# Head pair 0 of the first attention stage weighs its values in two halves of 128 tokens, and part of the early expert products is made from each half

## The chip, the cores and the metric

The kernel runs on one core of one Trainium2 chip. The metric is device microseconds (us) for one execution. Five engines work side by side, each through its own instructions in program order, and wait for each other through semaphores: PE (TensorE, matrix products), ACT (ScalarE), DVE (VectorE), POOL (GpSimd) and SP (SyncE, which here only issues DMAs). PE writes to PSUM; ACT and DVE read PSUM; the DMA queues move data between DRAM and SBUF.

## The reference, cut to what matters

Four batches of eight heads, 576 tokens, head width 64. Each query keeps its 32 best scores; the output feeds a mixture of eight experts whose gate is made doubly stochastic.

```
scores = q @ k.T / sqrt(64)                       # per batch and head, 576 x 576
keep the 32 largest per row, softmax over them    # attn
x = attn @ v                                      # 2304 x 512 after the heads are laid side by side
P = exp(x @ w_gate - max); 8 x: rows sum to 1, columns sum to 1, times N / E
out = sum over e:  P[:, e] * (relu(x @ w1[e]) @ w2[e])      # e = 0..7, 512 -> 1024 -> 512
```

Everything is float32. The row block of `x` that belongs to head pair `hp` (two heads, 128 columns) is `x[:, 128*hp : 128*hp + 128]`, so a product `x @ w1[e]` can be begun with the first head pair alone, as a sum over four such blocks.

## The kernel before, in words

Work is cut into blocks of 256 tokens. The attention of a block (a *stage*; the first is batch 0, tokens 0 to 255) goes head pair by head pair, `attend_heads`, L209, and inside a head pair by two *tiles* of 128 tokens, `weight_tiles`, L250: PE makes scores for each of the two heads (L122, L123, two matmuls for each half of the keys; the first tile of all in plain float32, L129), ACT copies them from PSUM (L134), DVE finds the 32nd largest by four MAX8 and three MATCH_REPLACE8 per head (L144, L147), ACT makes the exponentials (L150, L151), POOL and DVE normalise (L148, L199, L200, L203), PE transposes the weights in three groups of three blocks (L274) and ACT copies each group to the tile `at` (L291). When both tiles are in `at`, `weigh` (L301) multiplies by the values, 10 matmuls of 256 columns (L281), and ACT copies the result to `xt[:, hp, :]` (L304), from where it is split in a high and a low part (`xh` by ACT, L83; `xl` by DVE, L89).

Each expert product is made by three matmuls of such parts (L488 for the hidden layer, L601 for the outputs), and needs the block's four head pairs. To give PE something to do while the first stage is still under way, two functions make part of the hidden layer in plain float32 and store it in DRAM, where it is added later (`second_half`, L544):

- `first_quarter` (L516), called before head pair 1 is written out: for experts 4 to 7 the products with head pair 0 alone. For each expert four DMAs bring 128 rows of `w1` to a buffer `wr` (L520; three such buffers, `WR`, L48), and for each of four slices `s` two matmuls of 256 columns (L524) fill one bank of PSUM (`p1`, two buffers), ACT copies it to `y` (L512), SP stores `y` (L514).
- `first_half` (L528), called before head pair 2: for experts 0 to 3 the products with head pairs 0 and 1 (L537), four matmuls per slice.

Both are written at a low priority (`tc.high_priority(offset=-BIG)`, L367): a scheduler lays the instructions of each engine out in one fixed order before the run, by priorities and by a timeline of its own, and puts these matmuls where attention leaves PE free. Within an engine nothing overtakes at run time. After the first stage, `visit` (L567) takes one expert after the other over the blocks on board, and later attention stages are interleaved with it; `gate_logits` and `sinkhorn` make the gate; the last four blocks use a form with fewer products (L713, L775).

The names in the rows are tiles: `sp` scores in PSUM, `s` their copy, `m` the maxima, `Et` the weights, `pt` transposes or weighed values in PSUM, `p` a bank of expert products (`p_254` and the like in the lists of instructions: the stored part of one expert and slice), `raw`, `kh`, `kl`, `qs` the keys and queries, `wh`, `wl` weights in two parts.

Of the kernel before, what the change touches and what calls it, by code (L numbers as in the profile page):

```python
# [7 lines left out]
F32 = mybir.dt.float32  # L8
F32R = mybir.dt.float32r
U16 = mybir.dt.uint16  # L10
AF = mybir.ActivationFunctionType
# [4 lines left out]
DM, E, F = 512, 8, 1024  # L16
# [30 lines left out]
ALONE, LATER = range(0, 4), range(4, 8)  # L47
WR, WB, XR, NS, RAW, YB = 3, 6, 3, 3, 3, 4  # L48
# [3 lines left out]
def kernel(  # L52
# [11 lines left out]
    nc = tc.nc  # L64
    BIG = 1000000
# [3 lines left out]
    wp = ctx.enter_context(tc.tile_pool(name="wp", bufs=2))  # L69
    op_ = ctx.enter_context(tc.tile_pool(name="op", bufs=2))  # L70
# [3 lines left out]
    ps1 = ctx.enter_context(tc.tile_pool(name="ps1", bufs=2, space=PSUM))  # L74
# [3 lines left out]
    pst = actx.enter_context(tc.tile_pool(name="pst", bufs=2, space=PSUM))  # L78
    ap_ = actx.enter_context(tc.tile_pool(name="ap", bufs=2, side="right"))
    dram = ctx.enter_context(tc.tile_pool(name="dram", bufs=1, space=bass.MemoryType.DRAM))  # L80
# [35 lines left out]
    def scores(groups):  # L116
        sp = pss.tile([128, 2, 512], F32, name="sp")
        for dst, terms in groups:
            o = sp[:, dst[0], dst[1]:dst[2]]
            n = len(terms)  # L120
            for i, (qc, (kh, kl), cs) in enumerate(terms):
                nc.tensor.matmul(o, qc, kh[:, cs], start=(i == 0), stop=False)  # L122
                nc.tensor.matmul(o, qc, kl[:, cs], start=False, stop=(i == n - 1))  # L123
        return sp

    def plain_scores(qc, kr):
        sp = pss.tile([128, 2, 512], F32, name="sp")
        for a in range(2):
            nc.tensor.matmul(sp[:, a, 0:288], qc, kr[:, a * 288:a * 288 + 288], start=True, stop=True)  # L129
        return sp  # L130

    def copy_scores(sp):
        s = ap_.tile([128, S], F32, name="s", bufs=NS)
        nc.scalar.activation(s.rearrange("p (a b) -> p a b", a=2), sp, AF.Copy, scale=0.125)  # L134
        return s
# [111 lines left out]
        if not phases:  # L247
            attend_rest(hp, load_q("qm", 1024, 256, 1), ks, vr, xm)

    def weight_tiles(qs, ks, put, on_pool=False, crossed=None, plain=None):  # L250
        for t in range(2):
            Et = ap_.tile([128, 2, S], F32, name="Et", bufs=2)
            st = ap_.tile([128, 2, 2], F32, name="st", bufs=3)
            units = []
            for i in range(2):
                o = i * 256 + t * 128
                qc = qs[:, o:o + 128]
                if plain is not None and t == 0:
                    sp = plain_scores(plain[0][va if i == 0 else vb, o:o + 128], plain[1 + i][va if i == 0 else vb, :])
                else:  # L260
                    sp = scores([((a, 0, 288), [(qc, ks[i], slice(a * 288, a * 288 + 288))]) for a in range(2)])
                units.append((copy_scores(sp[:, :, 0:288]), Et[:, i, :], st[:, 0, i:i + 1]))
            topk(units, crossed is not None)
            normalise(Et, st, 2, on_pool)
            cs = slice(t * 128, (t + 1) * 128)
            if crossed is not None:
                cross(Et, crossed[:, :, cs])
                continue
            Ef = Et.rearrange("p a b -> p (a b)")
            for g in range(3):  # L270
                ps = pst.tile([128, 4, 128], F32, name="pt")
                for r in range(3):
                    j = g * 3 + r
                    nc.tensor.transpose(ps[:, r, :], Ef[:, j * 128:j * 128 + 128], idt)  # L274
                put(slice(g * 3, g * 3 + 3), cs, ps[:, 0:3, :])

    def weigh_values(av, vr, at, n, order):
        for j in order:
            for i, r in enumerate((va, vb)):
                o, block = (256 * i + 64 * j, 5 * i + j) if j < 4 else (512 + 64 * i, 4)  # L280
                weighed = nc.tensor.matmul(av[r, 0:n], vr[:, o:o + 64], at[:, block, 0:n], start=(j == order[0]), stop=(j == order[-1]))  # L281
        with tc.issue_after(weighed.ins):
            while ungated:
                gate_logits(*ungated.pop(0))

    def attend_phase(b, hp, qs, qm, ks, vr, xt, xm, plain=None):
        nq = 256 if xm is None else 320
        at = ap_.tile([128, 9, 320], F32, name="at", bufs=1)

        def put(blocks, cs, src):  # L290
            nc.scalar.activation(at[:, blocks, cs], src, AF.Copy)  # L291

        crossed = at if len(X) > 4 else None
        weight_tiles(qs, ks, put, b == 0 or crossed is not None, crossed, plain)
        if xm is not None:
            def put_rest(rows, blocks, src):
                nc.scalar.activation(at[rows, blocks, 256:320], src, AF.Copy)
            rest_weights(qm, ks, put_rest, None if crossed is None else at[:, :, 256:320])
        order = TAIL_FIRST if len(X) > 2 else range(5)

        def weigh():  # L301
            av = pst.tile([128, 512], F32, name="pt")
            weigh_values(av, vr, at, nq, order)
            nc.scalar.activation(xt[:, hp, :], av[:, 0:256], AF.Copy)  # L304
            if xm is not None:
                nc.scalar.activation(xm[:, hp, :], av[:, 256:320], AF.Copy)

        if turning:
            turning.append(weigh)
        else:  # L310
            weigh()
# [188 lines left out]


    PART = {}

    def half_weights(e, s2, half):
        wr = wp.tile([128, 2, 2, 256], F32, name="wr", bufs=WR)
        for r in range(2):
            nc.sync.dma_start(wr[:, r], w1[e, 2 * s2 + r, :, 2 * half:2 * half + 2, :])
        return wr

    def part(e, s, ps):  # L510
        y = op_.tile([128, 512], F32, name="y", bufs=YB)
        nc.scalar.activation(y, ps.rearrange("p a b -> p (a b)"), AF.Copy)  # L512
        PART[e, s] = dram.tile([128, 512], F32, name=f"p{e}_{s}")
        nc.sync.dma_start(PART[e, s], y)  # L514

    def first_quarter(x):  # L516
        for e in LATER:
            wr = wp.tile([128, 4, 256], F32, name="wr", bufs=WR)
            for s in range(4):
                nc.sync.dma_start(wr[:, s], w1[e, s, :, 0, :])  # L520
            for s in range(4):
                ps = ps1.tile([128, 2, 256], F32, name="p1")
                for fo in range(2):
                    nc.tensor.matmul(ps[:, fo, :], wr[:, s, fo * 128:(fo + 1) * 128], x[:, 0, :],  # L524
                                     start=True, stop=True)
                part(e, s, ps)
# [17 lines left out]
    def second_half(e, s, seat, wh, wl, k0):  # L544
        y = ap_.tile([128, 512], F32, name="yp", bufs=1)
        nc.sync.dma_start(y, PART[e, s])
        y = y.rearrange("p (a b) -> p a b", a=2)
# [333 lines left out]
```

## Time and profile before

| | us |
|---|---|
| median of 3 runs | 1831.21 (1831.04 to 1831.55) |
| profiled execution | 1833.39 |
| its span | 1831.6 |
| PE busy | 1785.6 (97%) |
| DVE, ACT, POOL busy | 1207.9, 1187.6, 1068.3 |
| DMA, mean rate | 148 GB/s |

The span runs from the first to the last instruction that the profiler recorded; 1.8 us of the profiled execution lie around it. A busy share is an average over stages. Two lines of the page cut the span in 40 slices of 45.8 us, each digit a tenth of busy time:

```
PE   4989999999999999999999999999999999999998
DVE  8999998988888878878787141255555555533333
```

Matmul durations overlap, since matmuls are pipelined; the pace of a run of equal matmuls is the distance of their starts. A row `x8` is eight matmul instructions; one float32 matmul of the code that has not been split in two parts is two instructions in the trace.

### The profile page before, as it was taken

How to read it: one execution, taken by the hardware profiler on the slowest of the kernel's cores; microseconds unless marked ns; L12 is line 12 of the kernel's file. 1: busy time of each engine (PE TensorE's matmuls, PEld its weight loads, DVE VectorE, ACT ScalarE, POOL GpSimd, SP SyncE). 2: the span in 40 equal slices, each digit the busy share in tenths (PEclk: the TensorE clock that was granted, in tenths of full speed). 3: DMA queues.
4: the chain of work that ended last, by engine and by line, in shares of the span. 5: the costliest groups of instructions: out<-in, count | busy, mean ns of one | idle time of the engine just before them, and what ended most of it. 6: DMA issues, size and time to landing. Idle time of an engine off the chain costs nothing.

```text
span 1831.6 us, 26304 instructions
## 1 busy us (share of the span) xinstructions
PE 1785.6 (97%) x9385; PEld 1480.7 (81%) x9385; DVE 1207.9 (66%) x2232; ACT 1187.6 (65%) x1785; POOL 1068.3 (58%) x842
## 2 busy tenths in 40 slices
PE   4989999999999999999999999999999999999998
PEld 3777888888888878777787889888888888888887
DVE  8999998988888878878787141255555555533333
ACT  5888899999999888988897645533333333333331
POOL 4367856656766585556564688955544554554441
PEclk9999999999999999999999999999999999999999
DMA  4885877765767575656655356423333333211111
GB/s 136 264 260 174 255 198 178 207 191 160 199 174 179 143 223 170 168 152 164 172 152 142 90 174 217 161 98 109 114 117 104 104 107 114 90 58 63 53 35 46
DMA packets 227203, 270.77 MB, mean 148 GB/s; under 512 B 142464, under 2 KB 146688, under 8 KB 227072
## 3 DMA queue, kind: packets, MB, share of 16 engines
q1 hardware_dynamic: 226928, 268.83, 49.8%
q8 instruction: 73, 1.20, 0.3%
q14 instruction: 58, 0.48, 0.1%
q10 hardware_dynamic: 144, 0.26, 0.0%
HBM read 202.19 MB, written 34.60 MB: 129 GB/s over the span
## 4 chain that ended last, share of the span: by engine, by line
PE 83%; ACT 4%; POOL 4%; DVE 3%; DMA 3%; issue 3%; SPq 0%; ACTq 0%; POOLq 0%
PE p L601 20%; PE p L775 19%; PE p L488 18%; PE p L713 10%; PE pc L713 5%; PE pt L281 4%; DMA wr<-in_w_dram 2%; PE pb L713 2%; POOL wl L86 2%; PE sp L122 2%; PE sp L123 2%; DVE m L144 1%; DVE w L147 1%; PE p L524 1%; ACT wh L83 1%
## 5 line engine op out<-in xcount | busy, mean ns | idle before, releaser
L86 POOL TENSOR_TENSOR wl<-wr,wh 128x1024 fp32r<-128x1024 f32 x288 | 694.0, 2422 | 456.2 <-ACT wh L83 445.7
L83 ACT ACTIVATE wh<-wr 128x1024 fp32r<-128x1024 f32 x288 | 304.1, 1061 | 284.4 <-PE p L713 191.2
L144 DVE MAX8 m<-w 128x8 f32<-128x576 f32 x432 | 320.6, 753 | 5.8
L488 PE MATMUL p<-xh,wh 128*128 128x256 f32 (+1 forms) x832 | 274.7, 330 | 2.8 <-DVE hl L557 1.9
L488 PE MATMUL p<-xl,wh 128*128 128x256 f32 (+1 forms) x832 | 273.7, 329 | 0.1
L488 PE MATMUL p<-xh,wl 128*128 128x256 f32 (+1 forms) x832 | 273.0, 328 | 0.0
L601 PE MATMUL p<-wh,hh 128*128 128x512 f32 x640 | 250.2, 396 | 4.3 <-ACT hh L556 2.8
L601 PE MATMUL p<-wl,hh 128*128 128x512 f32 x640 | 249.6, 392 | 0.0
L601 PE MATMUL p<-wh,hl 128*128 128x512 f32 x640 | 241.3, 392 | 0.0
L147 DVE MATCH_REPLACE8 w<-m,w 128x576 f32<-128x576 f32 x288 | 213.7, 743 | 0.0
L775 PE MATMUL p<-wh,h2h 128*128 128x512 f32 x512 | 199.1, 389 | 0.6 <-DVE acc L618 0.6
L775 PE MATMUL p<-wl,h2h 128*128 128x512 f32 x512 | 199.2, 389 | 0.0
L775 PE MATMUL p<-wh,h2l 128*128 128x512 f32 x512 | 196.3, 389 | 0.0
L618 DVE SCALAR_TENSOR_TENSOR acc<-p,P,acc 128x512 f32<-128x512 f32 x120 | 89.5, 750 | 160.4 <-PE p L775 160.4
L557 DVE SCALAR_TENSOR_TENSOR hl<-p,hh 128x512 fp32r<-128x512 f32 x160 | 109.0, 682 | 106.5 <-ACT hh L556 105.5
L488 PEld LDWEIGHTS p<-xh,wh 128*128 128x128 f32 x832 | 157.6, 189 | 20.8 <-issue 2.1
L488 PEld LDWEIGHTS p<-xl,wh 128*128 128x128 f32 x832 | 157.7, 189 | 15.7 <-issue 0.9
L488 PEld LDWEIGHTS p<-xh,wl 128*128 128x128 f32 x832 | 157.6, 189 | 14.2 <-issue 0.5
L144 DVE MAX8 m<-s 128x8 f32<-128x576 f32 x144 | 108.4, 753 | 85.3 <-ACT s L134 84.8
L601 PEld LDWEIGHTS p<-wh,hh 128*128 128x128 f32 x640 | 120.1, 188 | 31.7 <-ACT hh L556 5.3
L601 PEld LDWEIGHTS p<-wl,hh 128*128 128x128 f32 x640 | 120.6, 188 | 23.4 <-issue 0.4
L601 PEld LDWEIGHTS p<-wh,hl 128*128 128x128 f32 x640 | 119.9, 188 | 23.6 <-DVE hl L557 0.2
(171 smaller groups left out, 3550.4 us busy)
## 6 DMA issues: line engine op xcount, KB each, us to landing
wr<-in_w_dram SPq DMA_DIRECT2D x248, 512.0 KB, 3.5
y<-y SPq DMA_DIRECT2D x160, 256.0 KB, 2.8
raw<-in_k_dram SPq DMA_DIRECT2D x48, 288.0 KB, 3.7
p<-y SPq DMA_DIRECT2D x32, 256.0 KB, 4.0
wr<-in_w_dram SPq DMA_DIRECT2D x32, 256.0 KB, 4.3
yp<-p SPq DMA_DIRECT2D x32, 256.0 KB, 3.3
raw<-in_q_dram SPq DMA_DIRECT2D x31, 256.0 KB, 3.5
values<-in_v_dram SPq DMA_DIRECT2D x24, 256.0 KB, 3.6
```

The lines of the kernel that those rows point to most:

```text
L83: nc.scalar.activation(dst, src, AF.Copy)
L86: nc.gpsimd.tensor_tensor(dst, src, hi.bitcast(F32), op=OP.subtract)
L122: nc.tensor.matmul(o, qc, kh[:, cs], start=(i == 0), stop=False)
L144: nc.vector.max(m8[:, u, r, :], ws[u] if r else units[u][0])
L147: nc.vector.match_replace(ws[u], m8[:, u, r, :], ws[u] if r else units[u][0], LOWEST)
L281: weighed = nc.tensor.matmul(av[r, 0:n], vr[:, o:o + 64], at[:, block, 0:n], start=(j == order[0]), stop=(j == order[-1]))
L488: nc.tensor.matmul(ps[:, fo, :], a[:, kk, fs], x[:, k0 + kk, cs], start=(i == 0), stop=(i == 3 * nk - 1))
L557: nc.vector.scalar_tensor_tensor(seat.hl[:, ft, cs], src, 0.0, seat.hh[:, ft, cs].bitcast(F32), op0=OP.max, op1=OP.subtract)
L601: nc.tensor.matmul(ps, a[:, ft, ts], m[:, ft % 2, :], start=(i == 0), stop=(i == 3 * NFT - 1))
L618: return nc.vector.scalar_tensor_tensor(ACC[t], y, g, ACC[t], op0=OP.mult, op1=OP.add)
L713: nc.tensor.matmul(ps, w[:, kk, :], x[:, kk, :], start=(fresh and i == 0), stop=(i == 5), skip_group_check=True)
L775: nc.tensor.matmul(ps, a[:, ft, ts], m[:, ft, :], start=(i == 0), stop=(i == 11))
```

## The change

Only the call for the very first head pair changes (`plain is not None`), and the experts 5 to 7 of `first_quarter`.

- `weight_tiles` calls `then(t)` after each tile. In it, the values are weighed for that tile's 128 tokens alone (10 matmuls of 128 columns into a PSUM buffer of their own, in the order 0 to 4), and ACT copies 128 columns to `xt`. `weigh` is not called for this head pair.
- After tile 0, `first_eighths` loads the weights of experts 5, 6, 7 (the three `wr` buffers) and makes their products with the first 128 tokens: per expert two banks of PSUM with 8 matmuls of 128 columns, two copies by ACT, and four stores of 128 x 2 x 128 numbers, rows of 512 bytes.
- `first_quarter`, still called before head pair 1, makes the second 128 tokens of these three experts from the weights that are still in `wr`, then expert 4 as before.

```
+        if plain is not None:
+            def then(t):
+                av = pst.tile([128, 512], F32, name="pt")
+                weigh_values(av, vr, at, 128, range(5), t * 128)
+                nc.scalar.activation(xt[:, hp, t * 128:t * 128 + 128], av[:, 0:128], AF.Copy)
+                if t == 0:
+                    with tc.high_priority(offset=-BIG):
+                        first_eighths(xt)
+
+            weight_tiles(qs, ks, put, True, None, plain, then)
+            return
+        weight_tiles(qs, ks, put, b == 0 or crossed is not None, crossed)
...
+    QT = 3
...
+    SPLIT = []
+
+    def first_eighths(x):
+        for e in range(E - QT, E):
+            wr = wp.tile([128, 4, 256], F32, name="wr", bufs=WR)
+            for s in range(4):
+                nc.sync.dma_start(wr[:, s], w1[e, s, :, 0, :])
+            SPLIT.append((e, wr))
+            eighths(e, wr, x, 0)
+
+    def eighths(e, wr, x, t):
+        for s2 in range(2):
+            ps = ps1.tile([128, 2, 2, 128], F32, name="p1")
+            for r in range(2):
+                for fo in range(2):
+                    nc.tensor.matmul(ps[:, r, fo, :], wr[:, 2 * s2 + r, fo * 128:(fo + 1) * 128], x[:, 0, t * 128:t * 128 + 128],
+                                     start=True, stop=True)
+            y = op_.tile([128, 512], F32, name="y", bufs=YB)
+            nc.scalar.activation(y, ps.rearrange("p r a b -> p (r a b)"), AF.Copy)
+            for r in range(2):
...
+                nc.sync.dma_start(PART[e, 2 * s2 + r].rearrange("p (a b) -> p a b", a=2)[:, :, t * 128:t * 128 + 128],
+                                  y[:, r * 256:r * 256 + 256].rearrange("p (a b) -> p a b", a=2))
...
     def first_quarter(x):
-        for e in LATER:
+        for e, wr in SPLIT:
+            eighths(e, wr, x, 1)
+        for e in list(LATER)[:len(LATER) - QT]:
```

The scheduler lays all engines out anew. Three places show it; in these lists the number of matmuls is that of the code, and the lines of the changed kernel are 2 higher in `weight_tiles` and about 13 to 41 higher further down (L545 is the matmul in `eighths`, L283 the values, L548 the copy in `eighths`, L300 the copy to `xt` in `then`, L501 and L578 the matmuls that were L488 and L537).

PE before, from the last transposes of tile 0 of head pair 0 to the first values:

```order
L274 MATMUL pt<-idt,Et 128x128 x5
L122 MATMUL sp<-kh,qs 128x288
L123 MATMUL sp<-kl,qs 128x288
L122 MATMUL sp<-kh,qs 128x288
L123 MATMUL sp<-kl,qs 128x288
L274 MATMUL pt<-idt,Et 128x128 x9
L281 MATMUL pt<-at,values 64x256 x3
```

PE after, from the same transposes:

```order
L274 MATMUL pt<-idt,Et 128x128 x5
L283 MATMUL pt<-at,values 64x128 x10
L545 MATMUL p_196<-xt,wr 128x128 x4
L545 MATMUL p_207<-xt,wr 128x128 x4
L122 MATMUL sp<-kh,qs 128x288
L123 MATMUL sp<-kl,qs 128x288
L122 MATMUL sp<-kh,qs 128x288
L123 MATMUL sp<-kl,qs 128x288
L545 MATMUL p_223<-xt,wr 128x128 x4
L545 MATMUL p_234<-xt,wr 128x128 x4
L274 MATMUL pt<-idt,Et 128x128 x6
L545 MATMUL p_250<-xt,wr 128x128 x4
```

The values of tile 0 and 16 matmuls of the experts now stand between the transposes of tile 0 and those of tile 1, 8 of them ahead of the next scores.

ACT before, from the second weights of tile 1 of head pair 0 (`m_197`) to the scores of tile 1 of head pair 1:

```order
L150 ACTIVATE Et<-s,m_197 128x576
L151 ACTIVATE Et,st<-Et,eb 128x576 x2
L134 ACTIVATE s<-sp 128x576
L83 ACTIVATE kh<-raw 128x576
L83 ACTIVATE qs<-raw 128x512
L291 ACTIVATE at<-pt 128x3x128
L150 ACTIVATE Et<-s,m_420 128x576
L291 ACTIVATE at<-pt 128x3x128
L134 ACTIVATE s<-sp 128x576
```

ACT after, the same stretch (`m_290` and `m_468` are the same maxima):

```order
L150 ACTIVATE Et<-s,m_290 128x576
L300 ACTIVATE xt<-pt 128x128
L151 ACTIVATE Et,st<-Et,eb 128x576 x2
L134 ACTIVATE s<-sp 128x576
L548 ACTIVATE y<-p_196 128x512
L548 ACTIVATE y<-p_207 128x512
L83 ACTIVATE kh<-raw 128x576
L83 ACTIVATE qs<-raw 128x512
L548 ACTIVATE y<-p_223 128x512
L150 ACTIVATE Et<-s,m_468 128x576
L548 ACTIVATE y<-p_234 128x512
L293 ACTIVATE at<-pt 128x3x128 x2
```

One copy to `xt` stands ahead of the two L151, and four copies of expert products stand ahead of the next L134, which follows the last row shown.

PE before, where `first_half` ends and the first visit begins (head pair 3's values are the L281):

```order
L281 MATMUL pt<-at,values 64x256 x10
L537 MATMUL p_706<-xt,wr 128x256 x4
L122 MATMUL sp<-kh,qs 128x288
L123 MATMUL sp<-kl,qs 128x288
L122 MATMUL sp<-kh,qs 128x288
L123 MATMUL sp<-kl,qs 128x288
L274 MATMUL pt<-idt,Et 128x128 x3
L537 MATMUL p_715<-xt,wr 128x256 x4
L274 MATMUL pt<-idt,Et 128x128 x3
L488 MATMUL p_2844<-xh,wh 128x256
```

PE after, from the end of `first_half` on:

```order
L578 MATMUL p_763<-xt,wr 128x256 x4
L122 MATMUL sp<-kh,qs 128x288
L123 MATMUL sp<-kl,qs 128x288
L122 MATMUL sp<-kh,qs 128x288
L123 MATMUL sp<-kl,qs 128x288
L501 MATMUL p_2892<-xh,wh 128x256
L501 MATMUL p_2892<-xl,wh 128x256
L501 MATMUL p_2892<-xh,wl 128x256
L274 MATMUL pt<-idt,Et 128x128 x3
L283 MATMUL pt<-at,values 64x256 x3
```

The last of the early products now stands ahead of head pair 3's values, where before two groups of them stood behind.

## Rows read from the trace of the kernel before

**Rows 1.** The page, busy us of each engine, share of the span, instructions.
```profile
PE 1785.6 (97%) x9385; PEld 1480.7 (81%) x9385; DVE 1207.9 (66%) x2232; ACT 1187.6 (65%) x1785; POOL 1068.3 (58%) x842
```

**Rows 2.** Busy time by stretch: start:end, length, engines, granted clock, DMA share, GB/s.
```profile
30.40:44.40 14.00, 7.35 (x37) 4.70 (x37) 14.00 (x32) 9.84 (x21) 5.74 (x9) 1.00 0.29 81
44.40:70.50 26.10, 24.74 (x128) 19.86 (x129) 25.35 (x56) 22.23 (x47) 9.23 (x13) 0.93 0.74 244
70.50:118.40 47.90, 43.94 (x238) 35.99 (x236) 42.23 (x88) 38.21 (x76) 26.73 (x27) 0.96 0.85 275
118.40:160.00 41.60, 36.23 (x239) 29.73 (x239) 41.48 (x83) 34.32 (x64) 31.33 (x27) 0.93 0.65 213
160.00:800.00 640.00, 637.02 (x3811) 533.59 (x3808) 550.19 (x1087) 583.03 (x872) 417.54 (x361) 1.00 0.68 187
800.00:1600.00 800.00, 796.70 (x3909) 660.73 (x3910) 426.43 (x723) 417.00 (x586) 470.31 (x328) 1.00 0.43 130
```

**Rows 3.** PE in order of time: start, length, line, operation, count, idle before it.
```profile
29.09 1.27 PE L274 MATMUL pt<-idt,Et 128*128 128x128 f32 x5
...
34.70 0.61 PE L122 MATMUL sp<-kh,qs 128*128 128x288 f32 x1 [4.35 <-ACT s L134]
...
36.25 2.36 PE L274 MATMUL pt<-idt,Et 128*128 128x128 f32 x9 [0.22 <-POOL Et L203]
38.78 1.08 PE L281 MATMUL pt<-at,values 128*64 128x256 f32 x6 [0.16 <-ACT at L291]
...
44.41 0.40 PE L122 MATMUL sp<-kh,qs 128*128 128x288 f32 x1 [1.97 <-ACT s L134]
...
45.05 3.37 PE L524 MATMUL p<-xt,wr 128*128 128x256 f32 x8
...
57.31 1.89 PE L524 MATMUL p<-xt,wr 128*128 128x256 f32 x8
59.04 0.82 PE L274 MATMUL pt<-idt,Et 128*128 128x128 f32 x6
...
111.43 2.38 PE L281 MATMUL pt<-at,values 128*64 128x256 f32 x20
...
118.41 0.38 PE L488 MATMUL p<-xh,wh 128*128 128x256 f32 x1
```

**Rows 4.** ACT in order of time, same columns, around the first values.
```profile
31.83 0.77 ACT L150 ACTIVATE Et<-s,m 128x576 f32<-128x576 f32 x1 [0.94 <-DVE m L144]
32.51 0.76 ACT L151 ACTIVATE Et<-Et,eb 128x576 f32<-128x576 f32 x1
...
35.83 0.68 ACT L83 ACTIVATE kh<-raw 128x576 fp32r<-128x576 f32 x1 [1.18 <-PE sp L122]
...
38.62 0.65 ACT L134 ACTIVATE s<-sp 128x576 f32<-128x576 f32 x1
...
50.89 1.10 ACT L512 ACTIVATE y<-p 128x512 f32<-128x512 f32 x2
```

**Rows 5.** DVE in order of time, same columns.
```profile
40.09 0.74 DVE L144 MAX8 m<-s 128x8 f32<-128x576 f32 x1
...
89.26 0.76 DVE L144 MAX8 m<-s 128x8 f32<-128x576 f32 x1 [3.01 <-ACT s L134]
```

**Rows 6.** ACT in order of time, conversions of weights and head pair 3's values.
```profile
85.73 1.06 ACT L83 ACTIVATE wh<-wr 128x1024 fp32r<-128x1024 f32 x1 [3.65 <-DMA wr<-in_w_dram]
...
115.43 1.06 ACT L83 ACTIVATE wh<-wr 128x1024 fp32r<-128x1024 f32 x1 [2.91 <-DMA wr<-in_w_dram]
116.39 0.37 ACT L304 ACTIVATE xt<-pt 128x256 f32<-128x256 f32 x1
```

**Rows 7.** DMA issues: what, queue, count, KB each, median us to landing.
```profile
wr<-in_w_dram SPq DMA_DIRECT2D x16, 128.0 KB, 3.2
```

**Rows 8.** SP's queue in order of time: start, length with its waits, line, count.
```profile
31.28 7.36 SPq L230 DMA_DIRECT2D raw<-in_k_dram  x2
...
54.88 0.85 SPq L514 DMA_DIRECT2D p<-y  x2
```

More of the change, by code (lines that the diff above doesn't have):

```diff
@@ L248, in attend_heads, with weight_tiles @@
             attend_rest(hp, load_q("qm", 1024, 256, 1), ks, vr, xm)
-    def weight_tiles(qs, ks, put, on_pool=False, crossed=None, plain=None):
+    def weight_tiles(qs, ks, put, on_pool=False, crossed=None, plain=None, then=None):
         for t in range(2):
@@ L275, in weight_tiles, with weigh_values @@
                 put(slice(g * 3, g * 3 + 3), cs, ps[:, 0:3, :])
-    def weigh_values(av, vr, at, n, order):
+            if then is not None:
+                then(t)
+    def weigh_values(av, vr, at, n, order, c0=0):
         for j in order:
@@ L280, in weigh_values @@
                 o, block = (256 * i + 64 * j, 5 * i + j) if j < 4 else (512 + 64 * i, 4)
-                weighed = nc.tensor.matmul(av[r, 0:n], vr[:, o:o + 64], at[:, block, 0:n], start=(j == order[0]), stop=(j == order[-1]))
+                weighed = nc.tensor.matmul(av[r, 0:n], vr[:, o:o + 64], at[:, block, c0:c0 + n], start=(j == order[0]), stop=(j == order[-1]))
         with tc.issue_after(weighed.ins):
@@ L293, in attend_phase @@
         crossed = at if len(X) > 4 else None
-        weight_tiles(qs, ks, put, b == 0 or crossed is not None, crossed, plain)
+        if plain is not None:
[9 more added lines that the diff above has]
+        weight_tiles(qs, ks, put, b == 0 or crossed is not None, crossed)
         if xm is not None:
@@ L514, in part @@
         nc.sync.dma_start(PART[e, s], y)
+    SPLIT = []
[16 more added lines that the diff above has]
+            for r in range(2):
+                if (e, 2 * s2 + r) not in PART:
+                    PART[e, 2 * s2 + r] = dram.tile([128, 512], F32, name=f"p{e}_{2 * s2 + r}")
+                nc.sync.dma_start(PART[e, 2 * s2 + r].rearrange("p (a b) -> p a b", a=2)[:, :, t * 128:t * 128 + 128],
+                                  y[:, r * 256:r * 256 + 256].rearrange("p (a b) -> p a b", a=2))
     def first_quarter(x):
-        for e in LATER:
+        for e, wr in SPLIT:
+            eighths(e, wr, x, 1)
+        for e in list(LATER)[:len(LATER) - QT]:
             wr = wp.tile([128, 4, 256], F32, name="wr", bufs=WR)
```

## The prediction

> **What bounds the kernel now.** I read the page's busy shares first: PE 97% [rows 1], so the sum of what PE does and waits is the time. Then the busy time by stretch, to see where the 46 us that PE is not busy (1831.6 less 1785.6) lie [rows 2]. From 160 us to 1600 us PE is busy 1433.7 of 1440 us: there nothing but PE's own work counts, and all that a PE that arrives earlier needs is that the others keep up; DVE is busy 550 of 640 us in 160 to 800 and 426 of 800 after it, ACT 583 and 417. Between 30.4 and 44.4 us PE is busy 7.35 of 14.0, from 44.4 to 160 us 104.9 of 115.6; the last stretch, with the end of the run, is not touched. In these first 160 us DVE is the busy one (14.0 of 14.0, then 25.35 of 26.1, 42.23 of 47.9, 41.48 of 41.6): attention goes at DVE's pace, and PE fills up with early expert products. So the third view is PE in order of time [rows 3]: it stands idle for 4.35 us up to 34.70 and 1.97 us up to 44.41, both times for a copy of scores by ACT (L134), and the expert products begin only at 45.05, because they wait for head pair 0's two tiles. The change attacks these two gaps.
>
> One run stands for all numbers: the profiled execution took 1833.39 us, of which 1831.6 are the span; the median of the runs is 1831.21, 2.2 us less. I work out a difference on the trace and take it from the median.
>
> **Moved work: the gain.** Per 128 tokens an expert's quarter is 8 matmuls of the code, 16 instructions in the trace; three experts make 48 instructions that can run ahead of 44.41 instead of behind it. In full flow eight instructions of 256 columns take 59.04 - 57.31 = 1.73 us [rows 3], 0.216 each, so 0.108 for half the columns: 48 x 0.108 = 5.2 us. Before 44.41 there is room: 4.35 + 1.97 us idle, and half of head pair 0's value matmuls (about 1.2 of 2.4 us, rows of 20 in 2.38) moves from behind 38.78 to about 31 as well. So PE comes out of the early products 5.2 us sooner: **-5.2 us**.
>
> **Split matmuls: PE's extra.** The same columns are made by twice as many instructions: 96 of 128 columns for 48 of 256, and the weights are loaded twice. Streams alone say no extra (0.108 is half of 0.216). The nearest row with 128 columns and new 128 x 128 weights for each is the transposes, six in 0.82 us, 0.137 each, with the last one's full length in it [rows 3]: 96 x (0.137 - 0.108) = 2.8 us. I take 0, since the 0.82 holds a tail that a flow has once; ends 0 and +2.8. Less than nothing is excluded, as no column goes away. The values are 40 instructions of 128 columns for 20 of 256; they need the same columns: 0, with the same reason.
>
> The Trainium skill, page "TensorE: Matmul & The Clock Gate", section "Back-to-back issue gap", speaks against the change: it gives a sustained 81 ns per matmul at 128 columns and 131 at 512, so that narrow ones cost well over their share. An estimate from it: 98 at 256, two narrow for one wide 162, which makes 1.66 times of the 10.4 us that the three experts' 48 instructions take, +6.9 us. The trace's wide instruction (216 ns) and its transposes (at most 137) are far from such a ratio; that result is a rival below.
>
> **Moved on ACT: what hides it, and what not.** Six copies L548 come forward, 0.48 us each by the pair of L512 [rows 4], and the copy to `xt` is made in two pieces (one extra, 0.3 to 0.4). ACT is busy 9.84 of 14.0 us there [rows 2], so 3.2 us fit, but they stand in its order ahead of things that attention wants. The copy L300 stands ahead of the two L151. At PE's full pace the values of tile 0 (20 x 0.06 = 1.2 us) run 30.9 to 32.1, L150 ends at 32.5, L300 ends at 32.9: L151 comes 0.4 later than 32.51. Then two L548, keys, queries, L548, L150, L548 and two `at` copies follow before the L134 that stands at 38.62. Walked through with the rows' lengths (keys and queries 0.55 each, L150 0.68, `at` 0.4): scores end at 35.6, the keys' copy, at 35.83 before, starts at 36.0, L134 at 39.6, 1.0 later. Its copy ended at 39.27 and DVE took it up at 40.09 [rows 4, 5], a slack of 0.82. DVE is 0.2 late. At PE's slower pace (five transposes in 1.27 us at 29.09, nine in 2.36 at 36.25, about 0.25 each [rows 3]) the values take 2.4 us and the first 16 expert instructions 3.5, L151 slips by 1.2, and the same walk ends with L134 at 43.7, 5.1 us late, DVE 4.3 late. PE was quick at 38.78 after working since 34.70 with gaps of 0.2; in the new order it works from before 29.1 with only half a microsecond without work at 30.4, so it should be quick soon after 31. (The granted clock reads 1.00 over all of 30.4 to 44.4 [rows 2], though the pace is half in its first part; I go by the pace.) I take **+0.5**; ends 0 and 4.3. Behind 44.41 ACT has six such copies less, 2.9 us, in a stretch in which it is busy 22.23 of 26.1; I count no extra for it.
>
> **Stores, loads, SP.** 24 stores of 128 KB with rows of 512 bytes replace 12 of 256 KB with rows of 2 KB. Two issues take 0.85 us [rows 8], so SP spends about 12 x 0.43 = 5 us more, half of it before 44 us, where it mostly waits (7.36 us for two key loads, on POOL). The key and query loads of head pair 2 are now queued behind stores that wait for ACT's copies; by the walk above the second key load goes out at about 39, before at 38.6, and its converted keys are wanted after 50. The DMA engines are 0.29 busy in 30 to 44 [rows 2]. Nothing waits for the stores before the first visit. Expert 4's weights come when expert 5's buffer is free, about 47 to 48, landing 3.2 later [rows 7], at 51; PE gets there after six banks, 44.4 + 5.2 + some slow pace = 51. Cost 0; ends 0 and +1.
>
> **What is late next: head pair 3.** With early products used up 4.7 us sooner, PE comes to the first visit sooner, which needs head pair 3. Before, its values stood ahead of the last two groups of early products (111.43, L488 at 118.41); now they stand behind the last one (third pair of lists), so this cover is gone. In front of `xt` ACT stood 2.91 us for a weight's DMA at 115.43, as at 85.73 for 3.65 us, which cost DVE 3.01 us [rows 5, 6]. Those weights wait for `wr` buffers that early products free; if these end sooner, the loads start sooner, and `xt` of head pair 3 can be had 3 to 5 us sooner. At later equal points of attention (scores of the next stage's head pair 1 onward) the new order on PE has 4 to 6 us more work behind it than the old one. So I let the gain pass: 0; ends +4.7 (all lost) and -3 (DVE's stall of 3.01 goes too). Any change of the order past 200 us is worth nothing I can name.
>
> Sum: -5.2 + 0 + 0.5 + 0 + 0 = **-4.7 us**; the span would be 1826.9, the median **1826.5**. With the -3 for DVE and ACT's slip at 0.2: 1823.2.
>
> **The rivals.**
>
> 1. *The gain is lost at head pair 3* (1831.2). PE runs out of early products at about 113.7 and stands until `xh` and `xl` come at 118.4 as before. For it: the new order, in which scores, transposes and values lie between the last early product and the first visit's bulk. Against it: ACT's 2.91 us at 115.43 is a wait on a transfer, and DVE has 5.7 us without work in 70.5 to 118.4 [rows 2] that can shrink.
> 2. *ACT holds up DVE* (1835.5, slower). One mechanism: at PE's slow pace the copies of the first four banks, which stand ahead of L134, let DVE's next scores come 5.1 us late, beyond the slack of 0.82; DVE has no pause until 84 to win it back, each head pair is 4.3 later, and the first visit, for which PE has no cover left, begins 4.3 later: 1831.2 + 4.3. It decides from a slip of L134 above 0.82 us, and it is past 0.2% from a slip of 4.5. For it: PE is at the slow pace at 36.25, and again in 45.05 to 48.4 (eight instructions in 3.37 us) after an idle time of 1.97. Against it: the new order keeps PE at work from before 29.1.
> 3. *Narrow matmuls cost more than their columns* (1829.3 by the transposes' 0.137). The mechanism is the weight load of each instruction, which then sets the pace; only the nearest row's tail speaks for it. By the page above it would be 1833.4.
> 4. *More than the moved work is gained* (1823.2), as DVE's stall at 86 to 89 goes.
>
> That the change does not do what it says, I exclude: the list shows L545 ahead of tile 1's transposes.
>
> **How the numbers follow.** Forecast 0.50, rival 1 0.18, rival 2 0.13, rival 3 0.07, rival 4 0.12. About 0.2% (3.7 us) is what a measurement can tell from no change here. Within the forecast's own spread (1824 to 1829) 0.43 is beyond 3.7 us, 0.07 not; rival 4 adds 0.12 and rivals 1 and 3 together 0.04 to faster: 0.59. Same: 0.07, 0.15 of rival 1, 0.05 of rival 3, 0.02 of rival 2: 0.29. Slower: 0.11 of rival 2 and 0.01 of rival 3: 0.12. The range reaches from 1822.0 (rival 4 with one more microsecond) to 1833.0 (rival 1 with some of rival 2's slip); outside it lie most of rival 2 and a little of rival 4.
>
> **What would show it.** L545 starts at about 33 and its 48 instructions for tile 0 are done before 44; their starts are 0.11 apart in full flow (0.137 or more: rival 3). L134 for tile 1 of head pair 1 starts at 39 to 40 (43 or later: rival 2), and DVE has no gap over 0.5 us there. The first L578 comes 4 to 5 us ahead of where the first L537 was. The first visit's matmuls in flow come near 114 (118 or later with PE idle ahead of them: rival 1). In 160 to 1600 us PE's busy share stays as it is, with the whole shifted. It is wrong if the gaps of 4.35 and 1.97 us are filled, and the same time is idle between 100 and 160.

## The result: 0.7% slower, and the profile after

The changed kernel takes 1844.35 us (median of four runs, 1840.16 to 1848.88) against 1831.17 for the kernel before, run beside it: the ratio is 1.0073, 95% interval 1.0054 to 1.0092. (Ratios here are worked out over all runs of both kernels, so they can differ by up to 0.1% from those of the medians.) The forecast of 1826.5 with a range to 1833.0 does not hold it, and none of the four rivals does. The profiled execution is the one of 1848.88 us.

The page of the changed kernel, its span and the busy us of each engine:

```profile
span 1847.1 us, 26472 instructions
PE 1792.8 (97%) x9453; PEld 1486.7 (80%) x9453; DVE 1210.1 (66%) x2232; ACT 1189.1 (64%) x1786; POOL 1068.9 (58%) x842
```

PE is busy 7.2 us more than in [rows 1] and not busy 54.3 us, where it was 46. So of the 15.5 us by which the span is longer, 8.3 are idle time of PE and 7.2 are busy time: 68 more matmul instructions, and matmuls that take longer. Kernel e1 below, with the same 9453 matmul instructions in another order, is busy 1788.7 us, so about 4 of the 7.2 come with the order. The busy time by stretch, in the columns of [rows 2], says where:

```profile
30.40:44.40 14.00, 12.13 (x109) 10.41 (x107) 14.00 (x32) 12.83 (x29) 6.14 (x9) 1.00 0.43 118
44.40:70.50 26.10, 20.90 (x132) 16.32 (x133) 23.94 (x53) 20.08 (x42) 9.36 (x14) 1.00 0.81 241
70.50:118.40 47.90, 43.28 (x229) 34.88 (x229) 44.22 (x92) 38.95 (x75) 28.90 (x28) 0.96 0.87 285
118.40:160.00 41.60, 39.85 (x278) 33.40 (x275) 40.87 (x85) 35.48 (x67) 30.45 (x26) 1.00 0.62 193
160.00:800.00 640.00, 622.38 (x3639) 518.53 (x3638) 532.84 (x1047) 562.56 (x842) 403.44 (x348) 0.99 0.66 182
800.00:1600.00 800.00, 799.21 (x3974) 664.11 (x3973) 437.90 (x752) 430.70 (x608) 473.07 (x333) 1.00 0.45 134
```

The gap of 30 to 44 us is filled (12.13 for 7.35). In 118 to 160 PE does 3.6 us more; over the whole of 30.4 to 160 us it is busy 116.2 us where it was 112.3. Then 160 to 800, which had 3.0 us without PE, has 17.6. From about 1012 us before the change and 1028 after it, the last 3850 matmul instructions of the two traces stand in the same sequence of operations, tiles and shapes. The same one of them, before and after:

```profile
1012.64 0.39 PE L601 MATMUL p<-wh,hh 128*128 128x512 f32 x1
```
```profile
1028.53 0.39 PE L642 MATMUL p<-wh,hh 128*128 128x512 f32 x1
```

It is 15.9 us late, and the last of the 3850 is 16.2 us late: the whole loss is made ahead of this common tail. The early part itself went as forecast. PE in order of time, after the change:

```profile
33.59 2.05 PE L545 MATMUL p<-xt,wr 128*128 128x128 f32 x16 [0.80 <-ACT xt L300]
...
36.27 1.95 PE L545 MATMUL p<-xt,wr 128*128 128x128 f32 x16
...
38.71 1.97 PE L545 MATMUL p<-xt,wr 128*128 128x128 f32 x16
...
44.88 0.40 PE L122 MATMUL sp<-kh,qs 128*128 128x288 f32 x1 [1.55 <-ACT s L134]
```

All 48 instructions are done before 41, 0.11 to 0.13 apart; of the idle times of 4.35 and 1.97 us in [rows 3] 0.80 and 1.55 are left. What PE waits for in 160 to 800 us (total, times, longest), with 17.5 us in these rows:

```profile
PE p L501 <- DVE hl L598: 6.7, 7, 1.9
PE p L642 <- ACT y L650: 3.9, 3, 2.7
PE p L642 <- ACT hh L597: 3.1, 2, 2.1
PE p L642 <- ACT wh L83: 2.3, 2, 2.2
PE sp L122 <- ACT s L134: 1.3, 2, 0.8
...
```

These are results that ACT and DVE make for PE: the copy of a finished bank, the Relu and its low part, a converted weight. The longest wait, first on ACT, then on PE:

```profile
520.03 1.16 ACT L181 ACTIVATE halves<-Et 128x1152 uint16<-128x1152 uint16 x1 [1.09 <-DMA turned<-halves]
...
521.30 2.38 ACT L171 ACTIVATE at<-turned 128x2304 uint16<-128x2304 uint16 x1
523.59 0.76 ACT L151 ACTIVATE Et<-Et,eb 128x576 f32<-128x576 f32 x1
...
524.35 1.05 ACT L650 ACTIVATE y<-p 128x512 f32<-128x512 f32 x2
```
```profile
522.03 0.29 PE L123 MATMUL sp<-kl,qs 128*128 128x288 f32 x1
524.98 0.50 PE L642 MATMUL p<-wh,hh 128*128 128x512 f32 x1 [2.65 <-ACT y L650]
...
525.54 0.39 PE L642 MATMUL p<-wh,hl 128*128 128x512 f32 x1
525.77 0.40 PE L642 MATMUL p<-wh,hh 128*128 128x512 f32 x1
...
526.79 0.63 PE L642 MATMUL p<-wh,hh 128*128 128x512 f32 x1
527.22 0.63 PE L642 MATMUL p<-wl,hh 128*128 128x512 f32 x1
```

The two copies L650 that free PE's banks stand on ACT behind a copy of transposed weights (2.38 us) and an exponential. And the wait costs more than itself: PE starts at 0.23 apart up to 526, then at 0.43 for about eight matmuls.

### The profile page after: what moved, and what is told of

Read it like the earlier page. It is cut to its first block, busy times and chain, and to the rows that moved or that the text cites. A ratio compares the mean times of both kernels' runs of the same rounds, so it can differ in the third digit from the quotient of the medians.

```text
span 1847.1 us, 26472 instructions
## 1 busy us (share of the span) xinstructions
PE 1792.8 (97%) x9453; PEld 1486.7 (80%) x9453; DVE 1210.1 (66%) x2232; ACT 1189.1 (64%) x1786; POOL 1068.9 (58%) x842
## 4 chain that ended last, share of the span: by engine, by line
PE 73%; ACT 7%; DVE 7%; DMA 5%; POOL 4%; issue 4%; SPq 0%; ACTq 0%; POOLq 0%; DVEq 0%
PE p L816 19%; PE p L642 15%; PE p L501 15%; PE p L754 9%; PE pc L754 5%; PE pt L283 3%; DVE m L144 3%; DMA wr<-in_w_dram 3%; DVE w L147 2%; PE pb L754 2%; POOL wl L86 2%; PE sp L122 2%; PE sp L123 1%; ACT at L171 1%; ACT wh L83 1%
## 5 line engine op out<-in xcount | busy, mean ns | idle before, releaser
L501 PE MATMUL p<-xh,wh 128*128 128x256 f32 (+1 forms) x832 | 277.5, 334 | 7.7 <-DVE hl L598 6.7
L501 PE MATMUL p<-xh,wl 128*128 128x256 f32 (+1 forms) x832 | 274.9, 331 | 0.0
L501 PE MATMUL p<-xl,wh 128*128 128x256 f32 (+1 forms) x832 | 274.8, 330 | 0.0
L598 DVE SCALAR_TENSOR_TENSOR hl<-p,hh 128x512 fp32r<-128x512 f32 x160 | 108.9, 682 | 116.6 <-ACT hh L597 116.2
L501 PEld LDWEIGHTS p<-xh,wh 128*128 128x128 f32 x832 | 159.7, 192 | 26.5 <-DVE hl L598 7.8
L501 PEld LDWEIGHTS p<-xl,wh 128*128 128x128 f32 x832 | 159.8, 192 | 14.9 <-DVE xl L89 0.2
L501 PEld LDWEIGHTS p<-xh,wl 128*128 128x128 f32 x832 | 159.6, 192 | 14.3 <-issue 0.4
```

Source lines behind the costliest of these rows:

```text
L501: nc.tensor.matmul(ps[:, fo, :], a[:, kk, fs], x[:, k0 + kk, cs], start=(i == 0), stop=(i == 3 * nk - 1))
L598: nc.vector.scalar_tensor_tensor(seat.hl[:, ft, cs], src, 0.0, seat.hh[:, ft, cs].bitcast(F32), op0=OP.max, op1=OP.subtract)
```

## The experiments

The first theory (**A**): the scheduler's new order behind the first visit makes the loss. Its rival (**B**): PE arrives early and runs into ACT and DVE, whatever the order. To tell them apart the order was held. At the end of the kernel a list chains each engine's instructions, in issue order alone, to a recorded order:

```
+    for engine, rows in runs.items():            # recorded order, as positions in the order of writing
+        mine, prev = emitted[keys[engine]], None
+        for first, n in rows:
+            for t in range(first, first - n, -1):
+                ins = mine[len(mine) - 1 - t]
+                if prev is not None:
+                    tc.add_manual_dep(ins, prev.name, ...NoSync...)
+                prev = ins
```

Each ratio is to the kernel before on the same chip, whose median there was 1832.3 to 1833.1.

**e1**, the new early part with the old order on all five engines from the first visit (L488, now L501) on. Edit: the list, on the changed kernel.

> The changed kernel up to the first visit; from there on every engine (PE, ACT, DVE, POOL, SP) issues its instructions in the order of the kernel before, held by a list. Theory A (the loss lies in the new order of the instructions behind the first visit, which the scheduler chose): the early gain of 4 to 6 us stays, 1825 to 1828 us, and PE's busy time in 160 to 800 us comes back to about 637 of 640. Theory B (PE, being some 6 us ahead, runs into ACT and DVE, which are not ahead, whatever the order): no gain, 1831 to 1844, and PE idle for more than 10 us in 160 to 800.

1834.07 us, 1.0013 (1.0003 to 1.0024).

**e2**, the converse. Edit: the changed kernel's order as the list, on the kernel before.

> The kernel before up to the first visit; from there on every engine issues in the order of the changed kernel, held by a list. Theory A (the new order itself costs the time): the whole loss shows without the early gain, 1844.4 + 4 to 6 = 1848 to 1851 us, PE idle for more than 15 us in 160 to 800, and a spread from run to run of several us, as after the change. Theory B (the loss comes from PE being ahead): PE is not ahead here, so 1831 to 1834.

1847.06 us, 1.0085 (1.0071 to 1.0098). e1, then e2:

```profile
44.40:70.50 26.10, 22.38 (x131) 18.61 (x131) 23.05 (x52) 19.02 (x39) 9.21 (x13) 0.88 0.81 247
...
118.40:160.00 41.60, 36.62 (x232) 31.12 (x232) 41.02 (x81) 34.68 (x66) 28.91 (x24) 0.88 0.57 181
160.00:800.00 640.00, 637.35 (x3800) 534.05 (x3798) 550.91 (x1089) 585.09 (x872) 419.35 (x361) 1.00 0.67 188
```
```profile
160.00:800.00 640.00, 625.41 (x3680) 520.71 (x3679) 535.07 (x1057) 570.03 (x849) 409.62 (x352) 0.99 0.66 184
```

The waits go with the order, not with the early part: 2.7 us of 640 with the old order, 14.6 with the new one, where nothing was moved early. So the loss lies in the order, as A says, at 0.6 to 0.85%. But e1 is not the 1825 to 1828 that A expected: the early part alone makes 1.0013 in the old order. In the new order it makes 1.0073 / 1.0085 = 0.9988, from two chips and with intervals that overlap: about nothing.

**e3, e4, e11**: the change with 0, 2 and 1 experts in halves, order left to the scheduler.

```
-    QT = 3
+    QT = 0        # e3;  2 in e4, 1 in e11
```

> Head pair 0's values per 128 tokens as in the change, but no expert product is made from the first 128 tokens (QT = 0, the early quarters all per 256 tokens as before). Theory B (ahead): nothing moves on PE, so 1830 to 1832 us. Theory A (a new order, drawn anew by each edit): the order behind the first visit is again another, and the time follows it and not the work moved: anywhere in 1827 to 1850, with a difference from 1831 that PE's waits in 160 to 800 explain.

> The change with two experts in halves instead of three (QT = 2): 32 instructions moved into the early gaps instead of 48. Theory B (ahead): the loss is in proportion, 1831 + two thirds of 13 = about 1840 us. Theory A: the time does not follow the count; any value in 1826 to 1850, by the waits of its own order in 160 to 800.

> The change with one expert in halves (QT = 1, 16 instructions moved), order left to the scheduler: a further draw of an order. If each new order costs what it happens to cost: 5 to 25 us above the kernel before, not between QT = 0 (22 above) and QT = 2 (16 above) by rule. If the loss follows the work moved: between 16 and 22 above.

1854.22 (1.0118, 1.0103 to 1.0132), 1849.25 (1.0088) and 1848.52 us (1.0086). The kernel that moves no product early is the slowest, so the loss does not grow with the work moved, as B would have it. It falls from 1.18% to 0.73% as products of 0, 1, 2 and 3 experts are moved; whether that is a small gain or the luck of one order for each count, these runs do not tell, and e11, 15.7 us above, lies in the first of its expected bands and just below the second.

**e6**, e3 with the old order from the first visit on.

> Values per 128 tokens without early expert products (as in e3), and from the first visit on the order of the kernel before on every engine. If the order behind the first visit made the whole loss of e3: within 1.5 us of the kernel before. If the halved values cost by themselves (ten more matmuls, one more copy on ACT, attention late by it): 3 us or more above it.

1831.74 us, 0.9995 (0.9986 to 1.0003). The whole 1.2% of e3 was the order. And in the held order moving the products gains nothing: e1, which moves them, stands at 1.0013, e6, which does not, at 0.9995. e6 also shows that holding an order costs no time by itself.

**e7**, e1 with PE alone held.

> The changed kernel, in which PE alone follows the order of the kernel before from the first visit on; ACT, DVE, POOL and SP stay as the scheduler lays them around that. If the way in which attention and visits alternate on PE makes the loss: within 3 us of the kernel before. If it is the order on ACT and DVE (copies that PE waits for standing behind other work): 8 to 14 us above it.

1866.98 us, 1.0184 (1.0165 to 1.0203): some 34 us above, more than either expectation and worse than either full order. The order of PE alone does not bring the old time back. Which engine's order costs it does not show, since ACT, DVE and POOL issue here in neither the old order nor that of the changed kernel.

**e5**, the changed kernel's order up to 165 us, then the old one.

> The changed kernel's own order on every engine up to 165 us of its trace, where PE had done about 6 us more of the visits than before the change at the same progress of attention; from there the order of the kernel before, less what is already issued. Theory A (the lead is sound and only the later order gave it back): 4 to 6 us below the kernel before. Theory B (a lead of PE alone is worth nothing, since attention on DVE and ACT is not ahead, and PE meets it sooner and waits): within 2 us of the kernel before, with 5 us more of PE idle between 160 and 300 us.

1832.61 us, 1.0001 (0.9990 to 1.0011). The kernel before, then e5:

```profile
160.00:300.00 140.00, 139.37 (x914) 119.83 (x911) 132.65 (x270) 123.89 (x198) 99.61 (x84) 1.00 0.72 205
```
```profile
44.40:70.50 26.10, 21.32 (x121) 16.70 (x122) 23.02 (x51) 18.39 (x38) 8.98 (x14) 0.87 0.83 245
70.50:118.40 47.90, 43.34 (x223) 34.88 (x221) 41.85 (x86) 37.40 (x73) 26.27 (x26) 0.96 0.80 262
118.40:160.00 41.60, 38.88 (x268) 32.06 (x268) 40.82 (x86) 35.62 (x66) 30.26 (x26) 1.00 0.66 204
160.00:300.00 140.00, 135.59 (x888) 115.02 (x887) 134.17 (x273) 124.86 (x200) 100.38 (x86) 1.00 0.71 208
```

So no gain, as B expected. PE's lead at 160 is given back as 3.8 us more of waits before 300, for scores (1.9 us on L134) and for attention's weights (1.6 us on L203). Attention is not ahead: DVE, which carries it, is busy 105.7 us between 44.4 and 160, where it was 109.1 [rows 2].

**e8**, e1 with one store per bank.

```
-            for r in range(2): ... nc.sync.dma_start(PART[e, 2 * s2 + r]..., y[:, r * 256:r * 256 + 256]...)
+            nc.sync.dma_start(PAIR[e, s2]...[:, :, :, t * 128:t * 128 + 128], y...)
```

> As e1 (new early part, old order from the first visit on), but each bank of the halved products is stored by one transfer of 256 KB in place of two of 128 KB, so SP issues 12 stores in place of 24. In e1 ACT waited 3.5 us for a buffer y whose store was not done, near 60 us, and the copy of scores behind it came at 62.1 against 60.1 in the kernel before. If these stores are what takes e1's gain away: that copy at 58 to 60 and the time 2 to 3 us below e1. If not: as e1.

1832.60 us, 1.0005 (0.9995 to 1.0015). The copy of scores came at 61.0, with a wait of 1.55 for the store, not at 58 to 60; the intervals of e1 and e8 overlap, so neither expectation is decided. What the stores do shows in e1 itself, ACT and then DVE:

```profile
57.35 0.85 ACT L150 ACTIVATE Et<-s,m 128x576 f32<-128x576 f32 x1
60.91 1.27 ACT L526 ACTIVATE y<-p 128x512 f32<-128x512 f32 x2 [2.70 <-DMA p<-y]
62.07 0.65 ACT L134 ACTIVATE s<-sp 128x576 f32<-128x576 f32 x1
```
```profile
62.75 0.76 DVE L144 MAX8 m<-s 128x8 f32<-128x576 f32 x1 [1.79 <-ACT s L134]
```

All four `y` buffers waited for their stores, and ACT with them; this L134 stood at 60.14 before the change, and DVE lost 1.79 us.

**e10**, less PE work in the old order. One bank is made where there were four.

```
-                ps = ps1.tile([128, 2, 256], F32, name="p1")
-                for fo in range(2):
+                if s == 0:
+                    ps = ps1.tile([128, 2, 256], F32, name="p1")
+                for fo in range(2 if s == 0 else 0):
```

> The kernel before with every engine held to its own order, in which first_quarter leaves out 24 of its 32 matmuls (48 instructions at 0.216, 10.4 us of PE between 45 and 70 us; one bank is copied and stored four times in place of four banks). Theory C (attention over DVE sets the end of the first 160 us, PE has room): within 2 us of the kernel before, PE idle 8 to 10 us more before 118. Rival (PE is the bound there, and work moved off it early is worth its length, as the prediction said of 5.2 us): 6 to 10 us below.

1830.43 us, 0.9984 (0.9975 to 0.9992): 10.4 us of PE work are worth 2.9, between the two expectations. In 44.4 to 70.5 PE is busy 5.1 us less than in [rows 2], and the stretches behind it differ by at most 1.3 us:

```profile
44.40:70.50 26.10, 19.65 (x91) 14.27 (x92) 25.86 (x58) 23.33 (x50) 9.28 (x14) 0.80 0.77 257
```

The granted clock of this stretch is 0.80, where it was 0.93 [rows 2]: the matmuls that are left ran slower, so part of the work taken away came back as slower work, and the 2.9 us are not the price of room on PE alone.

**e9**, a shorter chain of attention in the old order: two conversions that stood waiting for their load on ACT go behind attention's work.

```
ACT   - wh, Et L150, Et L151, y, s L134        + Et L150, Et L151, y, s L134, wh
ACT   - wh, xt, xh, Et L150, y                 + xt, xh, Et L150, y, wh
POOL  - wl, st, Et, Et ; wl, eb                + st, Et, Et, wl ; eb, wl
```

> The kernel before with every engine held to its own order, but for two conversions of weights, which on ACT stood waiting for their load in front of attention's work (3.65 us up to 85.73, 2.91 us up to 115.43): the first goes behind the next four ACT instructions (the copy of scores L134 among them) and the second behind head pair 3's copy to xt and its three followers; on POOL the low parts of the two go behind L199 and L203, and behind L148. No work is removed. Theory C (in the first 160 us attention's chain over DVE sets the end, so what shortens it counts in full): DVE's waits of 3.0 us at 86 to 89 and 1.66 us at 115.6 to 117.2 go, 3 to 4.7 us below the kernel before. Rival (PE's work sets it, as the prediction said): PE's wait of 2.08 us at 88.7 goes, at most 2 us, more likely nothing.

1834.51 us, 1.0009 (1.0001 to 1.0017): no gain. The L134 of 88.59 in the kernel before came at 83.20, and ACT then stood for the next loads:

```profile
83.20 0.63 ACT L134 ACTIVATE s<-sp 128x576 f32<-128x576 f32 x1
...
89.28 1.06 ACT L83 ACTIVATE wh<-wr 128x1024 fp32r<-128x1024 f32 x1 [1.35 <-DMA wr<-in_w_dram]
...
99.59 1.06 ACT L83 ACTIVATE wh<-wr 128x1024 fp32r<-128x1024 f32 x1 [1.81 <-DMA wr<-in_w_dram]
```

**e12 and e13**, fewer and more bytes in the old order.

```
-        PART[e, s] = dram.tile([128, 512], F32, name=f"p{e}_{s}")
+        PART[e, s] = dram.tile([128, 512], BF16, name=f"p{e}_{s}")          # e12, y and yp alike
+        nc.sync.dma_start(dram.tile([128, 512], F32, name=f"again{e}_{s}"), y)   # e13
```

> The kernel before with every engine held to its own order; the 32 early part sums are written to DRAM and read back as bfloat16 (a rounding that the reference does not make), so their stores are 128 KB in place of 256 KB: 4 MB less of some 20 MB between 44 and 118 us, where the DMA engines are 0.74 to 0.85 busy and PE and ACT wait for loads of weights. Theory D (transfers set the pace of that stretch): the loads land sooner, ACT's waits of 3.65 and 2.91 us shrink, 3 to 6 us below the kernel before. Theory C (attention over DVE alone sets it): within 1 us.

> The kernel before with every engine held to its own order; each of the 32 early part sums is stored twice, the second time to a tile that nobody reads (8 MB more before 118 us, 32 more issues on SP). Theory D (transfers set the pace): 8 MB at some 300 GB/s is 27 us, of which the room of 0.15 to 0.3 in 44 to 118 us takes some 15: 8 to 15 us above the kernel before. Theory C: within 2 us.

1828.99 us, 0.9981 (0.9972 to 0.9991), and 1843.08 us, 1.0062 (1.0050 to 1.0075). e12, then e13:

```profile
44.40:70.50 26.10, 24.80 (x137) 20.02 (x137) 26.10 (x58) 23.44 (x49) 9.25 (x13) 1.00 0.65 195
70.50:118.40 47.90, 43.61 (x251) 36.10 (x250) 44.98 (x94) 41.13 (x82) 30.19 (x30) 1.00 0.74 237
```
```profile
44.40:70.50 26.10, 22.97 (x122) 17.95 (x123) 24.57 (x55) 21.46 (x45) 9.22 (x13) 1.00 0.88 317
70.50:118.40 47.90, 37.96 (x187) 30.59 (x185) 37.78 (x79) 34.52 (x68) 23.49 (x24) 0.89 0.96 331
```

Time follows the bytes in both directions: with half the store bytes the DMA share falls by 0.09 and 0.11 and DVE works 45.0 us of 47.9 instead of 42.2; with twice as many it is 0.96, and PE, ACT and DVE all do less. So transfers are part of the pace before 118 us, as D expected. e13 is the less clean of the two: it also adds 32 issues on SP, and a buffer `y` is free only after its second store, for which ACT waited 5.0 us in all before 160. e12 is the fastest complete version, 3.5 us below the kernel before, with a rounding that the kernel before has not.

**e14**, e8 with e12's stores; **e17**, e12 with e9's moves.

> e8 (early products from the first 128 tokens, one store per bank, old order from the first visit on), held to e8's order, with the part sums stored as bfloat16. Theory D: with transfers out of the way the change's early gain shows: 4 to 7 us below the kernel before and 2 to 3 below e12. Theory C (the gain has nowhere to go, since DVE's chain is no shorter): as e12 within 1 us.

> e12 and e9 together: the old order with part sums stored as bfloat16, and the two conversions of weights put behind attention's work. If e9 brought nothing because the loads were late anyway, the shorter chain shows once the stores are halved: 2 us or more below e12. If not: as e12 or 1 to 2 us above it, as e9 stood to the kernel before.

1830.02 us, 0.9986 (0.9977 to 0.9994), and 1832.45 us, 1.0001 (0.9991 to 1.0011). With fewer bytes the early products bring nothing either: e14 stands as e12, as C expected. And with e9's moves e12's gain is not seen, though e17 and e12 ran on two chips and their intervals touch; nothing speaks for late conversions.

**e15**, the changed kernel in its own order with ten moves on ACT and DVE at eight of its waits; **e16**, the changed kernel beside it. One of the ten:

```
ACT  - at<-turned L171, Et L151, y<-p L650 x2        + y<-p L650 x2, at<-turned L171, Et L151
```

> The changed kernel with every engine held to its own order, but for ten moves on ACT and DVE at eight of the places where its trace shows PE waiting in 160 to 800 us (1.86, 1.28, 2.08, 0.65, 0.98, 2.65, 2.16 and 1.35 us, 13.0 in all): there the instruction that PE waits for (a Relu to hh, a copy to y, a low part hl, a converted weight wh) goes ahead of one to three instructions that stand before it on its engine (a 2.4 us copy of transposed weights, conversions, exponentials, MAX8). PE's, POOL's and SP's orders stay. Theory A in its sharper form (the new order loses because what PE waits for stands behind longer work on in-order engines): most of the 13 us and of the slow pace behind them go, 8 to 14 us below the changed kernel of this call. Rival (the waits come from transfers or from attention being late, and turn up elsewhere): within 4 us of it.

> The changed kernel itself, so that e15 has its own on this chip: 12 to 14 us above the kernel before, as the first time.

1838.30 us, 1.0031 (1.0020 to 1.0043), and 1844.83 us, 1.0073 (1.0060 to 1.0086). e16, then e15:

```profile
160.00:800.00 640.00, 623.52 (x3662) 518.72 (x3661) 533.82 (x1054) 565.90 (x846) 407.17 (x350) 0.99 0.66 183
```
```profile
160.00:800.00 640.00, 628.00 (x3699) 522.91 (x3698) 538.56 (x1066) 572.75 (x856) 409.17 (x353) 1.00 0.67 185
```

Ten instructions passed over one to three others give back 6.5 us, over half of the loss, less than the 8 to 14 expected: PE waits 12.0 us instead of 16.5, some waits came back beside the old places (2.27 us at 306.00, now for L598). So the place of ten instructions on ACT and DVE is shown to make about half of the loss; that the rest is of the same kind is not shown.

## Why the prediction was wrong

- **The step that failed: "Any change of the order past 200 us is worth nothing I can name."** It was priced at 0 without an end. The order measured 0.60% (changed kernel against e1) to 0.85% (e2), 11 to 16 us. The sign to watch was written down, that PE's busy share in 160 to 1600 stays as it is: it fell from 1433.7 to 1421.6 us. The lists showed the first 120 us re-laid; in the traces PE, ACT, DVE and POOL stand in another order up to 1004 to 1012 us of the kernel before. With PE busy 99.5% of 160 to 800 there was almost nothing to win there and much to lose.
- **Moved work, -5.2: run as forecast, worth nothing.** The instructions ran where and as fast as said, and even so none of e1, e5 and e14 is faster than its partner without the moved work (e6, the kernel before, e12). The premise that from 160 us on "nothing but PE's own work counts" hides the rest: up to 300 us PE alternates with attention, and attention came no sooner. e10 gives the price of early PE work in the old order: 2.9 us for 10.4, with the slower clock in it. Rival 1 named the place ("The gain is lost at head pair 3"), though not the wait: in e1 the first visit begins at 121.05 instead of 118.41, behind a bank whose copy stood on ACT behind an exponential; `xl` was ready at 120.02.

```profile
121.05 0.38 PE L501 MATMUL p<-xh,wh 128*128 128x256 f32 x1 [2.01 <-ACT y L526]
```

In e1 the granted clock is also 0.88 in 44 to 70 and in 118 to 160, where it was 0.93. In e8 it is 1.00 and 0.96, and e8 gains nothing either. In the changed kernel the sign "The first visit's matmuls in flow come near 114" did not show: L501 starts at 113.36, three instructions at a time, and runs in flow from 125.62.

- **Split matmuls, 0: right.** 16 narrow instructions start at 36.27 and the transposes behind them at 38.05: 0.111 each, half of the 0.216 of wide ones, so rival 3 falls. By the estimate that the prediction made from the Trainium skill, page "TensorE: Matmul & The Clock Gate", section "Back-to-back issue gap", narrow ones would have cost 1.66 times as much; the trace does not agree.
- **ACT's slip, +0.5: within its ends.** L134 came at 40.11 for 38.62, of which 0.77 is a shift that the whole trace has from its first matmuls on; the slip of 0.7 stayed within the slack of 0.82, and DVE was busy 14.0 of 14.0. Rival 2 did not happen.
- **Stores, 0 with +1 at most: the reason was wrong.** "Nothing waits for the stores before the first visit" left out the four `y` buffers: ACT waited 1.66 us for a store up to 61.56 in the changed kernel and 2.70 in e1, and DVE behind it 0.55 and 1.79. What that costs in the end e8 does not settle.
- **The range.** 1822 to 1833 was made of bounds of the first 160 us alone. Four edits that let the scheduler lay the order anew (the change, e3, e4, e11) came out 0.7 to 1.2% slower, none faster. Held to the old order, two of these early parts stand within 0.13% (e1, e6). With four draws it stays open how rare an order as good as the old one is, and why the scheduler's own timeline prefers the new ones.

## What to carry to other kernels

Where a scheduler writes the order, an edit is two changes: the one in the diff, and a new order for everything behind it. Hold the old order behind the edit to measure the first by itself, and give the second a price and a direction of its own: where the present order leaves almost no waits, a new one can hardly win and can lose much. Before counting on work moved to an idle gap, take as much work away and see whether the end moves, and read the granted clock beside it: a PE that is 97% busy over the run can have room in the stretch that matters.

## What the runs showed of the hardware

- A wait can cost PE more than itself. Behind the 2.65 us up to 524.98 the starts go from 0.23 to 0.43 apart for some eight matmuls, 1.6 us more; in 520 to 540 us the granted clock is 0.91 after the change and 1.00 in e15, where this wait is gone:

```profile
520.00:540.00 20.00, 17.35 (x83) 13.05 (x83) 15.01 (x29) 17.39 (x31) 7.64 (x6) 0.91 0.44 134
```
```profile
520.00:540.00 20.00, 20.00 (x104) 15.52 (x103) 16.60 (x34) 19.71 (x36) 11.86 (x10) 1.00 0.56 172
```

- Under one order a delay stays about what it was: ACT's copies of finished outputs in e1 stand 2.1 us behind their counterparts before at 149 us, 1.6 at 870 and 2.0 at 1151. And the scatter of one kernel is not the same everywhere: the kernel before ran 1831.04 to 1831.55 in four runs beside the changed kernel, 1830.41 to 1835.07 in 17 runs on the chip of e1 to e4.
